# An S4 convolution block with a token-mixing MLP: the second token matrix and seven of eight pairs of the first in half-precision high and low parts, with a new order of all operations

## The chip, the cores and the metric

The kernel runs on one core of one Trainium2 chip. The core has a matrix engine (TensorE, PE in the profile, with its weight loads as PEld), a vector engine (VectorE, DVE), an activation engine (ScalarE, ACT), a general one (GpSimd, POOL) and SyncE (SP), which here only issues DMAs; sixteen DMA engines move the data. The metric is the device time of one execution in microseconds. It is the median of three runs.

## The reference, cut to what matters

The input `A_u` has 2048 tokens of 512 channels. It is normalized once, and the result goes two ways: through a long convolution along the tokens (an S4 layer, whose kernel is made from 128 complex states a channel), and through a mixer MLP whose first half mixes tokens by shifting.

```python
xn = layernorm(x)
s = irfft(rfft(pad(xn)) * rfft(pad(K))) + xn * Dskip      # K from A, B, C, log_dt
h = gelu(layernorm(xn) @ w1)                              # w1: 512 x 512
g0, g1, g2, g3 = h in four quarters of 128 channels, shifted by +1, -1, +2, -2 tokens
x1 = xn + concat(g0, g1, g2, g3) @ w2                     # w2: 512 x 512
h2 = gelu(layernorm(x1) @ w3) @ w4                        # 512 x 1376, 1376 x 512
out = x + s * silu(x1 + h2)
```

In this document w1 is the first token matrix and w2 the second.

## The kernel before, in words

**Tiling.** The tokens are dealt out in 16 steps of 128, so that a shift by one token is a change of the step: step `s` holds every sixteenth token from `s` on. `X` holds all 16 steps of 128 x 512 in SBUF as fp32 and is updated in place. Two neighbouring steps make a pair, and there are eight pairs.

**Token mixing** (`token_mixing`, line 1247). For each pair j, `ln_first` (1059) makes the statistics and normalizes the steps of `X`; `x_pair` (1080) scales them for the second normalization and brings them to channels by tokens; `h_pair` (1103) multiplies by w1 and applies the GELU; `u_stage1` (1125) does the first stage of the convolution's transform of the same steps and stores it to DRAM (`scr_Ud`). Pairs below `HF` (line 49, 4) work in fp32: TensorE transposes the scaled step `x2`, a copy brings it from PSUM to `xT`, and `w1s`, the raw w1, is the weight. The other pairs work in fp16: `x2` is cast to a high part, the rest `x2 - high` is the low part, a transposing DMA makes `xT`, and three matmuls stand for one product: high by high, high by low, low by high (`PASSES`, 839). For this `first_weights` (1030) squares w1, makes a power-of-two scale of it through TensorE and VectorE (`pow2_scale`, 978) and splits the scaled w1 into `w1h`. The GELU results of all pairs are kept in fp32 in `hT`; `wrapped` (1146) makes the six blocks `hw` whose shift leaves the step range.

`hs_pair` (1159) then does two steps at a time: four fp32 matmuls of 128 x 128 by 128 x 512 a step (`hT` or `hw` with the raw w2, `w2s`), and VectorE adds the sum from PSUM to `X` and takes the statistics of the result.

**The MLP** (`mlp`, 1203) runs over eight pairs in `MLP_ORDER` and six blocks of w3 columns (2 x 128, the last 96). It always works in fp16 parts: a matmul group of 12 into bank `pb`, the GELU into `g32`, a high part (`E.affine`) and a low part (`scalar_tensor_tensor`) into `ghl`, and groups of 6 into bank `pa`, which collect w4's products of the pair. `prep` splits w3 and w4, whose scales come from `weight_scales` (1020).

**The convolution.** `tables` (818) builds the convolution kernel K for 32 channels at a time, 16 times: exponentials, sines and cosines on ScalarE (`waves`), large products on VectorE (`sums`), matmuls, and the first stage of its transform (`ks`), which is stored to DRAM as `scr_Kfa` (channels 0 to 255) and `scr_Kfb` (256 to 511) through one buffer, `k1e`. `products` (841) takes half of the channels at a time: loads `cst` (transform constants), `uin` and `kin`, does the second stage, multiplies the spectra, goes one stage back and stores `scr_Zda` or `scr_Zdb`. For the second half both inputs are split into fp16 parts (`uh`, `kx`; stages `uhalf` and `khalf`). It needs all of `scr_Kfb`. `inverse` (947) loads these as `zin`, does the last stage and multiplies it into `X`, which `gate` (941) has passed through SiLU; `finish` adds the residual `xr` and stores the output.

**What sets the order.** No loop order is kept. Every operation is recorded with its number, in the order in which the source makes it (`Plan.new`, 249); operations inside `together` count as one. The text `ORDER` (116 to 199) lists all 1952 numbers, and `Plan.issue` (327) issues them in that order, each to its engine, where they run in order. Operations made by `E` (`Either`, 409) can run on ScalarE or VectorE; a letter behind the number says which (`a` or `v`). In this list MLP groups, tables, products and token mixing are woven into one another. Since all operations are issued from one place, almost every row of the profile has line 330, and rows are told apart by their tiles. Tiles come from rings and fixed places of SBUF: `wtile` (four buffers of 2 KB) serves `x2`, `x2h`, `x1n`, `x1h` and `g32`, and a new tile in a buffer waits for the readers of the old one.

Of the kernel before, what the change touches and what calls it, by code (L numbers as in the profile page):

```python
# [19 lines left out]
P = 128  # L20
L = 2048
D = 512
# [26 lines left out]
HF = 4  # L49
# [67 lines left out]
23 20 21 0 22 39 7 8 1 6 5 105 86 3 2 106 107 108 109 110 111 112 87 89 88 90 113 91 114 115a 92 93 94 95 25 24  # L117
26 27 116a 96 97a 1070 98v 117a 120v 99v 100 101a 102v 103 118 172 170 4 168 171 169 173 9 104a 10 19 18 11 28
166 167 174 175 176 121 123 124 177 178 122v 119a 125 145 44 179 180v 183v 146 46 126 127 128 181a 147 47 48
187a 208a 142 31 29 30 182v 129 78 205a 130 148 79a 153a 184v 228 229 230 131 143 160 185 35 34 33 32 132 232  # L120
133 149v 154a 231 144 186a 188 134 552 226 189a 233 193 150a 227 234 235 135 236 237 194 161 196 190 293 553 295
294 291 238 14 292 297 155 156 13 16 15 191 239 298 296 138a 240 299 244v 300 140a 301 202a 242a 302 141 554
241v 303 201a 49 245v 50 209 195 206 52 51 304 246a 247 53 54 192 152 17 151 380 382 203 249a 214 207a 250a 197a
198a 305 215 211 212 12 199 204 200 157 251 139 56 216 55 210a 59 45 80 217 243v 57 555 381 307a 272a 213 383 58
60 253 254 306a 81a 61 164 218a 62 36 252 223a 219a 384 248 308v 273v 222a 158 63 274 255 67 268v 162 68 64 256
257 220 225 259 276 221 224 275 565 277 314v 269a 69 270 70 136 137 71 557 258 65 261a 260a 279 265a 315v 278 66
264a 316 388 309v 72 280 282 73 271 337v 310a 311v 74 84 312 262 263 281 284v 283v 318 75 560 562 319 333v 317
266 267 338v 287a 76 339 313 288a 77 321 322 85v 334v 323 324 335 285 286 42 82 586 558 320 344 83a 345 556 385
559 566 567 340 326a 325a 289 346 389 336 341 290 330a 329v 43 37 328 327 568 359 360 587 561 347 588 331 349v
571 159 348v 40 332 163 353v 352v 350 351 361 375 378 446 374 570 448 390 342 355 569 377 572 449 563 564 362  # L130
354 41 363v 394 592 468 450 364a 589 438 591 386 590 391 470 471 396 439 574 573 440 343 576 575 387 443 454 577
578 595 593 165 441 579a 395 367a 397 392 356 376 357 456 455 400 402 607 393 594 404 608 442 358 366 398 457
580 472 581 582a 583a 597 459 584 403 596 613 372 609 401 447 368a 369 451 399 416 610 611 460 598 452 599 405
417 444 365 406 371 435 418 585 612 600a 628 370 616 629 458 630 469 473 419 474 601 38 407 475 453 462 432 614
631 633 632 480 495 602 420 408 603a 604a 461 615 409 634 421 410 445 411 379 499 476 605 606 657 412 618 422
413 477 617 478 414 373 482 423 637 424 479 425 494 481 463a 544a 635 433a 545a 464 415 619 620 502 621a 485
548a 549a 546 636 622 426 491 434 649 428 550 436a 650 496 659 660 547 465 466a 503 517 516 437 639 654 521 651
504 661 638 430 551 467 653 652 492a 746 623 747 488 489a 518 507 624a 490 662 748 510 493 655 513 749a 861 753
# [293 lines left out]
def kernel(  # L432
# [814 lines left out]
    def token_mixing():  # L1247
        V.memset(ssq, 0.0)
        for j in range(8):
# [16 lines left out]
            if j == 0:  # L1266
                for k in range(3, 6):
                    wrapped(k)
# [90 lines left out]
```

## Time and profile before

| | |
|---|---|
| median of three runs | 536.88 us (535.1 to 538.08) |
| span of the profiled execution | 536.6 us |
| busy: TensorE, VectorE, ScalarE | 516.5, 489.8, 425.2 us |
| ACT_TABLE_LOAD on ScalarE | 52, 66.7 us |
| DMA | 93.50 MB, mean 174 GB/s |
| granted TensorE clock, mean | 0.994 |

In a row of groups stand the line, the engine and the operation, then the tiles (written<-read), partitions x elements and type, the count; behind the first bar the busy time in us and the mean ns of one; behind the second bar the idle time of the engine just before them and what ended it. In the chain of work that ended last a piece has its start, its length and what it was; in a table of stages each engine's busy time stands with its number of instructions, then the granted TensorE clock, the mean share of the DMA engines that was busy, and the rate.

### The profile page before, as it was taken

What the parts mean: (1) busy time and instruction counts of PE and PEld (TensorE: products, weight loads), DVE (VectorE), ACT (ScalarE), POOL (GpSimd) and SP (SyncE); (2) the same over time, 40 slices, a digit from 0 to 9 for tenths busy, and PEclk for the clock granted to TensorE, in tenths of its full rate; (3) what the DMA queues carried; (4) which work ended last, traced back from release to release, by engine and by line L of the source; (5) the groups of instructions that cost most, each with busy time, mean ns of one, the idle gap of its engine ahead of it and who ended that gap; (6) DMA issues with size and microseconds to landing.
All of it is one profiled execution on the core that took longest, in us unless ns stands there. A gap on an engine that the chain in (4) does not pass through costs nothing.

```text
span 536.6 us, 13619 instructions
## 1 busy us (share of the span) xinstructions
PE 516.5 (96%) x5628; PEld 332.4 (62%) x5628; DVE 489.8 (91%) x755; ACT 425.2 (79%) x692; POOL 0.7 (0%) x6
## 2 busy tenths in 40 slices
PE   8999999999999999999999999999899899999992
PEld 7787664554475766565765666575565667666631
DVE  4999999999999999999999999999877799997277
ACT  3999999899899999999799897868646566774340
POOL 0000000000000000000000000000000000000000
PEclk9999999999999999999999999999999999999997
DMA  8989975689677325356375738838889969896997
GB/s 228 214 268 257 230 200 155 190 132 127 158 188 118 46 36 60 42 68 112 120 137 148 150 108 167 145 94 176 149 170 169 348 201 297 261 280 226 314 277 205
DMA packets 212830, 93.50 MB, mean 174 GB/s; under 512 B 163297, under 2 KB 196065, under 8 KB 212385
## 3 DMA queue, kind: packets, MB, share of 16 engines
q1 hardware_dynamic: 208032, 88.18, 71.3%
q10 hardware_dynamic: 4736, 4.46, 2.8%
q8 instruction: 44, 0.72, 0.6%
q14 instruction: 18, 0.14, 0.1%
HBM read 56.96 MB, written 29.36 MB: 161 GB/s over the span
## 4 chain that ended last, share of the span: by engine, by line
PE 63%; DVE 12%; ACT 11%; DMA 7%; issue 3%; SPq 1%; DVEq 0%; ACTq 0%
PE pb L330 24%; PE pa L330 17%; PE pd L330 11%; PE pc L330 11%; DVE wv L330 4%; DMA scr_Kfb<-k1e 3%; DVE X L330 3%; ACT wv L330 2%; ACT mag L330 2%; ACT L330 2%; SPq L330 1%; DMA kin<-scr_Kfb 1%; DMA scr_Kfa<-k1e 1%; DMA cst<-c_gq 1%; ACT g L330 1%
## 5 line engine op out<-in xcount | busy, mean ns | idle before, releaser
L330 PE MATMUL pb<-x1T,w3h 128*128 128x256 f16 (+1 forms) x1056 | 125.1, 273 | 1.2 <-ACT g L330 1.2
L330 PE MATMUL pa<-w4h,ghl 128*128 128x512 f16 (+1 forms) x528 | 123.2, 380 | 0.0
L330 PEld LDWEIGHTS <-w3h 128*128 128x128 f16 (+1 forms) x1056 | 102.3, 100 | 27.8 <-issue 11.0
L330 PEld LDWEIGHTS <-ghl 128*128 128x128 f16 (+1 forms) x528 | 49.3, 98 | 59.1 <-issue 8.7
L330 ACT ACT_TABLE_LOAD x52 | 66.7, 1283 | 2.0 <-PEq L1347 1.2
L330 ACT ACTIVATE wv<-wv 128x2080 f32<-128x2080 int32 x32 | 63.0, 1968 | 0.3 <-DVE wv L330 0.3
L330 ACT ACTIVATE g<-pb,wsc 128x512 f32<-128x512 f32 (+1 forms) x48 | 30.6, 651 | 12.8 <-PE pb L330 11.5
L330 ACT ACTIVATE ghl<-g,wsc 128x512 f16<-128x512 f32 (+1 forms) x39 | 26.6, 688 | 13.3 <-PE pa L330 8.3
L330 DVE TENSOR_TENSOR wv<-wv,eg 128x2048 f32<-128x2048 f32 x16 | 36.5, 2284 | 0.1
L330 DVE TENSOR_TENSOR wv<-mag,wv 128x2048 f32<-128x2048 f32 x16 | 36.6, 2285 | 0.0
L330 PE MATMUL pd<-pr,cst 64*128 64x256 f32 x256 | 36.3, 402 | 0.0
L330 PEld LDWEIGHTS pc<-wv 128*32 128x32 f32 x2048 | 29.8, 109 | 9.7 <-issue 6.2
L330 PE MATMUL pc<-wv 128*32 128x64 f32 x2048 | 32.5, 220 | 2.7 <-issue 1.9
L330 DVE SCALAR_TENSOR_TENSOR ghl<-g,wsc,ghl 128x512 f16<-128x512 f32 (+1 forms) x48 | 33.5, 701 | 1.0 <-ACT ghl L330 0.8
L330 ACT ACTIVATE wv<-wv,halfpi 128x2080 f32<-128x2080 f32 x16 | 32.9, 2056 | 0.1
L330 ACT ACTIVATE mag<-par 128x128 f32<-128x128 f32 x132 | 32.8, 441 | 0.0
L330 ACT ACTIVATE kh<-pc,ksc 128x256 f32<-128x256 f32 (+1 forms) x40 | 20.1, 553 | 14.1 <-PE pc L330 12.5
L330 PEld LDWEIGHTS pd<-pr,cst 64*128 64x128 f32 x256 | 22.0, 186 | 11.5 <-issue 8.3
L330 PE MATMUL pb<-xT,w 128*128 128x256 f32 x128 | 29.0, 382 | 0.0
L330 PEld LDWEIGHTS pb<-xT,w 128*128 128x128 f32 x128 | 23.8, 190 | 5.5 <-issue 1.6
L330 PE MATMUL pb<-w,hT 128*128 128x512 f32 x58 | 26.9, 599 | 0.0
L330 DVE BATCH_NORM_STATS2 stats<-X 128x6 f32<-128x512 f32 x32 | 21.4, 681 | 5.3 <-DMA X<-in_A_u_dram 5.3
(167 smaller groups left out, 882.7 us busy)
## 6 DMA issues: line engine op xcount, KB each, us to landing
wst<-in_B_w_dram SPq DMA_DIRECT2D x20, 512.0 KB, 4.0
scr_Ud<-ue SPq DMA_DIRECT2D x32, 256.0 KB, 3.2
scr_Kfa<-k1e SPq DMA_DIRECT2D x16, 256.0 KB, 6.2
uin<-scr_Ud SPq DMA_DIRECT2D x16, 256.0 KB, 4.1
cst<-c_gp SPq DMA_DIRECT2D x16, 256.0 KB, 3.5
kin<-scr_Kfa SPq DMA_DIRECT2D x16, 256.0 KB, 3.6
scr_Zda<-z1e SPq DMA_DIRECT2D x16, 256.0 KB, 3.0
scr_Kfb<-k1e SPq DMA_DIRECT2D x16, 256.0 KB, 6.0
```

Of the source, the lines that this page charges most:

```text
L330: ins = [getattr(self.engines[op.eng], name)(*args, **kw).ins for name, args, kw in op.calls]
```

## The change

`HF` goes from 4 to 1, so that pairs 1 to 3 also run in fp16 parts. The input's parts are made straight from `X`: the high part is the scaled step written as fp16, the low part one `scalar_tensor_tensor` from `X`; the fp32 `x2` remains for pair 0 only. Each GELU block of `h_pair` goes to a scratch tile `h32` in the ring `wtile`, and its high and low fp16 parts (scaled by `sh`) go to `hT`, which keeps its size; `hw` likewise. `second_weights` scales and splits w2 into `w2h`, whose raw copy is loaded into two slots of `sblocks` instead. `hs_pair` does 12 fp16 matmuls a step in place of 4 in fp32, and its add to `X` also takes the scale back. Steps 0 and 1 are loaded and normalized singly. With 56 operations more (2008), `ORDER` is a new list throughout, in which the letters differ as well: of the operations that may run on either engine, copies to `ue` on VectorE are 1 (before: 9), to `kh` 2 (11), to `z1e` 10 (17), normalizations of `X` 3 (9).

```diff
-HF = 4
+HF = 1
...
-23 20 21 0 22 39 7 8 1 6 5 105 86 3 2 106 107 108 109 110 111 112 87 89 88 90 113 91 114 115a 92 93 94 95 25 24
...
+12 2 3 27 0 90 8 7 5 6 25 91 92 93 94 26 95 24 115 4 117 118 116 119 120 10 23 48 13 121 96 122 97 98 11 9 100 123 124
+101 102 22 50 99a 109v 110 103 104 125 14 134 135 105 51 52 106 107 111a 136 137 17 20 126a 82 108a 56 138 112a 139 19
...
-    hw = at(gtile.o, [P, 6, P], F32, "hw")
+    hw = at(gtile.o, [P, 6, 2, P], F16, "hw")
...
     def loads():
...
-        by_r(X[:, 0:2], xv[:, :, 0:2], load=(Q, A))
+        by_r(X[:, 0:1], xv[:, :, 0:1], load=(Q, A))
+        by_r(X[:, 1:2], xv[:, :, 1:2], load=(Q, A))
...
-        load_w(w2, w2s, w2place, Q)
+        load_w(w2, w2s, Slots(sblocks + 10 * K4, sblocks + 11 * K4), Q)
...
         for r in range(4):
...
-    s3, i3, s4, i4, sg, ig, a3, a4, s1, i1, a1 = [wsc[:, k : k + 1] for k in range(11)]
+    s3, i3, s4, i4, sg, ig, a3, a4, s1, i1, a1, s2, i2, a2, sh = [
+        wsc[:, k : k + 1] for k in range(15)
+    ]
...
     def weight_scales():
...
-        pow2_scale(ssq[:, 8:16], s4, i4, 2.0 ** 14)
+        pow2_scale(ssq[:, 8:14], s4, i4, 2.0 ** 14)
...
-    w1h = []
+    w1h, w2h = [], []
...
     def first_weights():
...
+        V.tensor_scalar(sh, s1, 2.0 ** -10, None, op0=ALU.mult)
         for k in range(2):
...
+    def second_weights():
+        due("wq2")
+        for k in range(2):
+            w = wides[2 + k]
+            A.activation(at(phB + 4 * K4, [P, 2, D], F32, "sq"), w, AF.Square, accum_out=ssq[:, 14 + k : 15 + k])
+        pow2_scale(ssq[:, 14:16], s2, i2, 2.0 ** 14)
+        V.tensor_scalar(a2, i2, i1, 2.0 ** 10, op0=ALU.mult, op1=ALU.mult)
+        for k in range(2):
+            w = w2place([P, 2, 2, D], F16, "w2h")
+            E.affine(w[:, :, 0], wides[2 + k], s2)
+            V.scalar_tensor_tensor(w[:, :, 1], wides[2 + k], s2, w[:, :, 0], op0=ALU.mult, op1=ALU.subtract)
+            w2h.append(w)
...
     def prep(jp):
...
         for i in range(2):
...
-            x2 = wtile([P, D], F32, "x2")
-            E.affine(x2, X[:, s], r12[:, s, 1:2])
+            r2 = r12[:, s, 1:2]
...
-                E.copy(xh[:, 0], x2)
-                V.tensor_sub(xh[:, 1], x2, xh[:, 0])
+                E.affine(xh[:, 0], X[:, s], r2)
+                V.scalar_tensor_tensor(xh[:, 1], X[:, s], r2, xh[:, 0], op0=ALU.mult, op1=ALU.subtract)
...
+            x2 = wtile([P, D], F32, "x2")
+            E.affine(x2, X[:, s], r2)
...
                 for k in range(4):
...
     def h_pair(j):
-        h = stile([P, 4, 2, P], F32, "hT")
+        h = stile([P, 4, 2, 2, P], F16, "hT")
...
         for m2 in range(2):
...
-            hv = h[:, 2 * m2 : 2 * m2 + 2].rearrange("p m a t -> p m (a t)")
-            A.activation(hv, ph, AF.Gelu_apprx_tanh, scale=1.0 if j < HF else a1)
+            hv = [h[:, 2 * m2 : 2 * m2 + 2, k].rearrange("p m a t -> p m (a t)") for k in range(2)]
+            h32 = wtile([P, 2, 2 * P], F32, "h32")
+            A.activation(h32, ph, AF.Gelu_apprx_tanh, scale=1.0 if j < HF else a1)
+            E.affine(hv[0], h32, sh)
+            V.scalar_tensor_tensor(hv[1], h32, sh, hv[0], op0=ALU.mult, op1=ALU.subtract)
...
     def u_stage1(s):
...
     def wrapped(k):
...
-        src, dst = hT[s // 2][:, m, s % 2], hw[:, k]
+        src, dst = hT[s // 2][:, m, :, s % 2], hw[:, k]
...
-            V.tensor_copy(dst[:, 32:P], src[:, 0:96])
-            V.tensor_copy(dst[:, 1:32], src[:, 96:127])
-            V.memset(dst[:, 0:1], 0.0)
+            V.tensor_copy(dst[:, :, 32:P], src[:, :, 0:96])
+            V.tensor_copy(dst[:, :, 1:32], src[:, :, 96:127])
+            V.memset(dst[:, :, 0:1], 0.0)
...
-            V.tensor_copy(dst[:, 0:96], src[:, 32:P])
-            V.tensor_copy(dst[:, 96:127], src[:, 1:32])
-            V.memset(dst[:, 127:P], 0.0)
+            V.tensor_copy(dst[:, :, 0:96], src[:, :, 32:P])
+            V.tensor_copy(dst[:, :, 96:127], src[:, :, 1:32])
+            V.memset(dst[:, :, 127:P], 0.0)
...
     def hs_pair(s0, k):
...
                 for m in range(4):
...
-                        w = hT[t // 2][:, m, t % 2]
+                        w = hT[t // 2][:, m, :, t % 2]
...
-                    T.matmul(acc[i], w, w2s[m], start=m == 0, stop=m == 3)
+                    for n, (lh, lw) in enumerate(PASSES):
+                        T.matmul(
+                            acc[i], w[:, lh], w2h[m // 2][:, m % 2, lw],
+                            start=m == 0 and n == 0, stop=m == 3 and n == 2,
+                        )
         for i in range(2):
...
-            V.tensor_add(X[:, s], X[:, s], acc[i])
+            V.scalar_tensor_tensor(X[:, s], acc[i], a2, X[:, s], op0=ALU.mult, op1=ALU.add)
...
         for j in range(8):
...
             if j == 0:
-                ln_first(slice(0, 2))
+                ln_first(slice(0, 1))
+                ln_first(slice(1, 2))
...
             if j == 0:
                 for k in range(3, 6):
...
+        second_weights()
         for k in range(3):
...
         for i in range(12):
...
```

More of the change, by code (lines that the diff above doesn't have):

```diff
@@ L122 @@
[L122 to L131, printed above, removed]
@@ new lines @@
+1348 760 1362 576 761 543 762 1349 1363 1357 1367 1379 732a 565 1380 557 1368a 1369 746 1374a 763 1375 733 1364 1370
+747 749 734 1371 764 903 704 735a 736a 737 1376 738 765 750 769 766 1377 751 592 752 781 753a 754 1386 1387 593 594
+596 755 1381 1382a 1388 1389a 1378 756a 757a 758 595 782 1400a 1383 1401a 783 767 759 1390 1393 1394 1395 768 1408
+1409 1384 1402 784 1385 1415 785 1396a 1404a 786 1391 770 771 772 773 1392 774a 1397 597 1403 787 790 775 776 1405a
+788 1127 1406 1410 1128 789 1416 777a 1129 1411a 1131 778a 780 1412 1417 1422 791 1398 1399 1423 1413 1414 1137 1138
@@ L199 @@
+1900 1902 1908 1926 1951 1911 1598 1599 1905 1907 1968 1615 1605 1616v 1610v 1611 1617 1887 1914 1916 1906 1606 1915
[4 rows of a table added]
 """
```

132 lines of the change are left out of this document (65 added, 67 removed), and 11 rows, old and new, of the table ORDER.

## The prediction

> **What bounds the kernel now.** I read the page's busy times first, then the busy times by stage, then the chain that ended last.
>
> ```profile
> PE 516.5 (96%) x5628; PEld 332.4 (62%) x5628; DVE 489.8 (91%) x755; ACT 425.2 (79%) x692; POOL 0.7 (0%) x6
> ```
>
> TensorE is the fullest engine, VectorE is close behind, and an average over the span can't say which of them sets the end. So the stages:
>
> ```profile
> core 0: us, PE busy (x) PEld busy (x) DVE busy (x) ACT busy (x) POOL busy (x), PEclk, DMA share, GB/s
> 0.00:20.00 20.00, 17.09 (x117) 16.00 (x118) 12.25 (x46) 10.61 (x19) 0.70 (x6) 1.00 0.95 236
> 20.00:100.00 80.00, 79.05 (x629) 53.70 (x628) 78.02 (x152) 79.56 (x141) 0.00 (x0) 1.00 0.79 209
> 100.00:406.70 306.70, 302.15 (x3686) 187.28 (x3684) 298.70 (x397) 266.16 (x425) 0.00 (x0) 1.00 0.66 125
> 406.70:418.80 12.10, 12.06 (x92) 8.04 (x90) 6.21 (x22) 6.79 (x10) 0.00 (x0) 1.00 1.25 219
> 418.80:489.00 70.20, 68.78 (x703) 47.28 (x703) 65.61 (x88) 48.43 (x86) 0.00 (x0) 1.00 0.84 264
> 489.00:536.60 47.60, 37.40 (x410) 20.08 (x407) 28.97 (x55) 13.63 (x15) 0.00 (x0) 0.93 0.91 267
> 418.00:422.00 4.00, 2.63 (x29) 1.60 (x30) 3.64 (x5) 2.39 (x4) 0.00 (x0) 1.00 1.01 398
> 504.00:508.00 4.00, 4.00 (x30) 2.90 (x29) 0.28 (x1) 1.99 (x3) 0.00 (x0) 1.00 1.11 334
> 528.00:532.00 4.00, 0.99 (x16) 0.31 (x16) 3.96 (x10) 0.00 (x0) 0.00 (x0) 0.79 0.81 233
> ```
>
> Up to 406.7 us, where the last store of the convolution's stage-one spectrum is issued (the front), TensorE and VectorE are both over 97% busy, and from 20 to 100 us ScalarE is too. From 418.8 to 489 (the second half's products) TensorE is full with VectorE behind it. Behind 489 (the tail) TensorE still has MLP groups, and the transfers run at a share of 0.91. Between front and products stands a chain of transfers:
>
> ```profile
> 394.40 6.44 DMA scr_Kfb<-k1e
> ...
> 402.93 9.37 DMA scr_Kfb<-k1e
> ...
> 412.35 5.86 DMA kin<-scr_Kfb
> ```
>
> Its 12.1 us are spent in TensorE on MLP groups, which is why the TensorE share hides it.
>
> **TensorE: what goes.**
>
> ```profile
> L330 PE MATMUL pb<-xT,w 128*128 128x256 f32 x128 | 29.0, 382 | 0.0
> L330 PE MATMUL pb<-w,hT 128*128 128x512 f32 x58 | 26.9, 599 | 0.0
> L330 PE MATMUL pa<-w,hT 128*128 128x512 f32 x58 | 26.1, 594 | 0.0
> L330 PE MATMUL pb<-xT,w1h 128*128 128x256 f16 x192 | 22.0, 272 | 0.6 <-ACT hT L330 0.3 <-DMA xT<-x2h 0.3
> L330 PE MATMUL pd<-ident,x 128*128 128x128 f32 x32 | 4.3, 278 | 1.6 <-DVE x L330 1.3 <-ACT xT L330 0.2
> L330 PE MATMUL pa<-w,hw 128*128 128x512 f32 x6 | 3.1, 592 | 0.0
> L330 PE MATMUL pb<-w,hw 128*128 128x512 f32 x6 | 3.1, 592 | 0.0
> ...
> L330 PE MATMUL pa<-w4h,ghl 128*128 128x512 f16 x480 | 111.8, 380 | 0.0
> ```
>
>
> The second token matrix takes 26.9 + 26.1 + 3.1 + 3.1 = 59.2 us in fp32. In three half-precision passes it is 16 steps x 12 matmuls; at the MLP's 111.8 / 480 = 0.233 us for the same shape that is 44.7 us: 14.5 less. A pair of the first matrix is 29.0 / 4 = 7.25 us in fp32 and 22.0 / 4 = 5.5 us in fp16; three pairs change: 5.2 less. Of 32 transposes 24 go: 3.2 less. The new scale of w2 adds three instructions, under 1 us. TensorE ends 22 us lighter, at about 494.
>
> **VectorE and ScalarE: what comes.**
>
> ```profile
> L330 DVE SCALAR_TENSOR_TENSOR ghl<-g,wsc,ghl 128x512 f16<-128x512 f32 x40 | 29.7, 745 | 0.9 <-ACT ghl L330 0.8
> L330 ACT ACTIVATE ghl<-g,wsc 128x512 f16<-128x512 f32 x33 | 23.8, 722 | 13.3 <-PE pa L330 8.3 <-DVE X L330 3.4 <-DMA cst<-c_gq 1.4
> L330 DVE TENSOR_SCALAR ghl<-g,wsc 128x512 f16<-128x512 f32 x7 | 3.3, 477 | 0.9 <-PE pa L330 0.9
> L330 DVE SCALAR_TENSOR_TENSOR w1h<-w,wsc,w1h 128x1024 f16<-128x1024 f32 x2 | 2.6, 1280 | 0.0
> L330 ACT ACTIVATE w1h<-w,wsc 128x1024 f16<-128x1024 f32 x2 | 2.2, 1134 | 0.0
> L330 ACT ACTIVATE sq<-w 128x1024 f32<-128x1024 f32 x2 | 2.1, 1064 | 0.0
> L330 DVE TENSOR_SCALAR wsc<-wsc 128x1 f32<-128x1 f32 x10 | 1.5, 146 | 0.0
> L330 DVE TENSOR_TENSOR x2h<-x,x2h 128x512 f16<-128x512 f32 x8 | 5.5, 689 | 0.0
> L330 DVE CAST x2h<-x 128x512 f16<-128x512 f32 x5 | 2.1, 423 | 0.0
> L330 ACT CAST x2h<-x 128x512 f16<-128x512 f32 x3 | 1.8, 616 | 0.0
> L330 ACT COPY xT<-pd 128x512 f32<-128x512 f32 x7 | 3.9, 590 | 0.7 <-PE pd L330 0.7
> L330 DVE COPY ue<-pa 128x512 f32<-128x512 f32 x6 | 4.0, 685 | 0.0
> L330 DVE TENSOR_SCALAR X<-X,rs,bs 128x512 f32<-128x512 f32 x9 | 4.8, 543 | 0.1
> L330 DVE TENSOR_SCALAR kh<-pc,ksc 128x256 f32<-128x256 f32 x7 | 3.2, 476 | 0.2 <-ACT kh L330 0.2
> L330 DVE COPY z1e<-pd 128x256 f32<-128x256 f32 x17 | 7.0, 420 | 2.7 <-PE pd L330 2.7
> ```
>
> Each of the 16 GELU blocks of h_pair now gets a high part and a low part. The MLP's ghl is the same form: low parts 16 x 0.745 = 11.9 us on VectorE; high parts, by the letters in the order, 10 on ScalarE (7.2) and 6 on VectorE (2.9). For w2: low parts 2 x 1.28 = 2.6, high parts about 2.2, squares 2.1, and some ten one-column steps at 0.146, 1.5. Inputs of the first matrix: 14 low parts at 0.745 come (10.4); 8 subtractions (5.5), 8 casts (3.9) and 6 copies of xT at 0.59 (3.5) go: 2.5 less. The add in hs_pair takes a scale along: up to 1 us in all, taken as 1. Sum: 11.9 + 10.1 + 8.4 - 2.5 + 1 = 29 us, all ahead of the last table, where both engines are full. The letters push other work to ScalarE: off VectorE go 8 ue (5.5), 6 X (3.3), 9 kh (4.3), 7 z1e (2.9) and a few more, so VectorE gains only about 5 and ScalarE 24. The two single first steps should let the first normalization begin about 1 us earlier (0 to 2).
>
> **What the order moves.**
>
> ```profile
> 505.95 1.29 PE pa L330 x6
> 507.25 1.31 PE pb L330 x12
> ```
>
> ```profile
> L330 ACT ACTIVATE X<-X 128x1024 f32<-128x1024 f32 x8 | 8.3, 1053 | 4.9 <-DVE X L330 4.8
> ```
>
> Each number in ORDER is an operation in the order in which the source makes them, so the two lists can be read by stage. 47 MLP matmul groups (of 12 or 6 matmuls) stand behind the last spectrum store before and 23 after. A group in a row of groups takes about 1.3 us in the chain. So the front gets 24 groups, 31 us of TensorE, and with them 7 GELUs, 6 high and 6 low parts (19 at some 0.7: 13 us), four gates at 1.05 (4.2) and eight steps of norm and add near 0.7 (5.6): 23 us of VectorE and ScalarE.
>
> Front, before: VectorE 12.25 + 78.02 + 298.70 = 389, ScalarE 356, TensorE 398 us busy. After: TensorE 398 - 22 + 31 = 407; VectorE and ScalarE together 745 + 29 + 23 = 797, by the letters 405 and 392. VectorE still leads. At the 97.5% that 78.02 of 80 shows, the front takes 20 + (405 - 12.3) / 0.975 = 422.8 us; the same sum for before gives 406.4, as measured. Less the earlier start: 421.8, so 15 us **later** than now.
>
> New waits stand in the front too. Pairs 1 to 3 now need w1's scaled parts and a transposing DMA each where they needed copies of xT; in TensorE's list the next pairs and the u_stage1 blocks are queued behind them, and ScalarE's GELUs wait for those. hs_pair needs the scale of w2, a chain of small steps between VectorE and TensorE, with the updates of X behind it. I cost these at nothing because TensorE has room: its own sum for the front is 20 + (407 - 17.1) / 0.988 (79.05 of 80) = 414.6, 8 us ahead of VectorE's. Beyond 8 us of stall, or where VectorE is starved by one, each us counts in full. Six more transposing DMAs and four more X loads pass through SP's queue ahead of the stores of u and the later weight loads; the front's transfer share of 0.66 to 0.79 leaves room.
>
> Middle: the last store and load set it, with five groups beside them in both lists: 12.1 us, unchanged (a store alone took 6.44 or 9.37, so 3 us either way). Products: 22 groups stand there before, 8 after: TensorE 68.8 - 18 = 51, VectorE 65.6 - 11 = 54.5 (their splits and adds). At VectorE's present 65.61 / 70.2 that is 58.5 us. The transfers (264 x 70.2 = 18.5 MB) would need 311 GB/s; the best row has 398. I take 59.5. Tail: 10 groups in place of 20: TensorE 37.4 - 13 = 24, off the path. What remains is 267 x 47.6 = 12.7 MB; at the 334 GB/s of 504 to 508 that is 38.0; I take 38.5.
>
> Sum: 421.8 + 12.1 + 59.5 + 38.5 = 531.9 against the span of 536.6, or 4.7 less; on the median of 536.88 that is **532 us**.
>
> **The rivals.**
> *Slower: the transfers take TensorE's place.* Behind 418.8 the kernel moves 31.2 MB. My forecast wants 98 us for it, 318 GB/s on average. For it speak 398 and 334 GB/s in single rows; against it that whole stages ran at 264 and 267 with shares of 0.84 and 0.91, so full shares would give only 314 and 293, or 59 + 43 us. If the rates stay as they are, 421.8 + 12.1 + 117.8 = 552; halfway, 542. It turns into a loss where the average stays under 31.2 MB / 102.7 us = 304 GB/s. The Trainium skill ("DMA: Bandwidth & Descriptors", "Where 436 GB/s comes from") puts the HBM limit of one core at about 358 GB/s; by that figure 31.2 MB would need 87 us at least, and the 398 of 418 to 422 stands above it. Chance 0.22.
> *No change: an even trade.* Full shares, 102 us, just pay for the front: 536. Chance 0.20.
> *Much faster: the front does not grow.* If VectorE's and ScalarE's additions fell into gaps, TensorE's 22 us would come off: 514. Against it: VectorE's 97.5% from 20 us on. Chance 0.04.
> *A cold TensorE.* In the tail TensorE will have 24 us of work in 38.5, so it idles in pieces. The row of 528 to 532, where it is idle three parts in four, shows a granted clock of 0.79. Were it at half the clock for the whole tail, its 24 us would be 48, 9.5 past the tail: 541. Against it: 14 us of idle time in many pieces leave few of several us. The Trainium skill ("TensorE: Matmul & The Clock Gate", Part 1) says that an idle window of about 3.4 us halves the clock; that row agrees in direction. Chance 0.04.
>
> **How the numbers follow.** My forecast has 0.50. About 0.5% is what a measurement of this kernel can tell from no change, 534.2 to 539.6 us. Forecast and much faster lie under it: 0.54. Above lie the transfer case and the cold one: 0.26. The even trade is the same: 0.20. The range: at 99% for VectorE, as ScalarE's 79.56 of 80, the front is 416 and the end 526; with the tail at 398 GB/s (32 us) 520. Above, the transfer case halfway, 542, and a front at 96%, 6 us more on my forecast, 538. I take 521 to 543.
>
> **What would show it.** Right: TensorE about 494 busy, VectorE 494, ScalarE 449; the last store of the spectrum near 422 us; from there under 111 us with GB/s above 310; in the late chain VectorE and DMA in place of TensorE's pa and pb. Wrong: the store before 415 or behind 430 (the sum of the front), a late part of 118 us or more at the old rates (the transfers), or TensorE still filling the products.

## The result, and the profile after

The changed kernel takes 564.45 us (median of 4 runs, 562.69 to 568.28) beside 537.48 us for the kernel before (4 runs, 535.1 to 540.35): a ratio of 1.050, 95% interval 1.044 to 1.056. It is **slower by 27 us**. The forecast was 532 us, its range 521 to 543.

The page of the changed kernel, first busy time by engine, then the stages (columns as in the tables above). The stages are cut as in the prediction: where the issue of the last `scr_Kfb` store ends, at 443.1 us (before: 406.9); the cuts are 442.9 and 406.7.

```profile
PE 508.9 (90%) x5719; PEld 329.5 (58%) x5719; DVE 496.1 (88%) x764; ACT 451.2 (80%) x735; POOL 0.7 (0%) x6
```

```profile
core 0: us, PE busy (x) PEld busy (x) DVE busy (x) ACT busy (x) POOL busy (x), PEclk, DMA share, GB/s
0.00:20.00 20.00, 15.85 (x98) 14.55 (x99) 11.37 (x43) 11.62 (x19) 0.70 (x6) 0.94 0.90 227
20.00:80.00 60.00, 51.90 (x434) 36.74 (x434) 51.01 (x118) 49.17 (x82) 0.00 (x0) 0.91 1.03 246
80.00:100.00 20.00, 20.00 (x132) 12.72 (x130) 19.86 (x40) 19.09 (x46) 0.00 (x0) 1.00 0.73 211
20.00:100.00 80.00, 71.90 (x563) 49.47 (x563) 70.87 (x157) 68.25 (x127) 0.00 (x0) 0.93 0.96 237
100.00:442.90 342.90, 330.65 (x4102) 211.05 (x4099) 325.31 (x433) 314.77 (x492) 0.00 (x0) 1.00 0.57 113
442.90:456.10 13.20, 10.18 (x67) 5.16 (x65) 9.87 (x24) 6.68 (x8) 0.00 (x0) 1.00 1.06 233
456.10:520.50 64.40, 54.11 (x588) 37.51 (x592) 53.34 (x63) 41.00 (x84) 0.00 (x0) 0.97 0.85 269
520.50:564.30 43.80, 26.19 (x318) 11.76 (x312) 25.36 (x48) 8.86 (x9) 0.00 (x0) 0.76 0.97 287
```

Two things are to be seen. The busy times of VectorE (496 for 494) and ScalarE (451 for 449) are close to the forecast's: their work was counted rightly. TensorE's 509 for 494 is 15 us more; its granted clock is 0.91 to 0.97 in the rows up to 80 us and in the products, and 0.76 in the tail. But from 20 to 100 us no engine is full any more. Before, VectorE was busy 97.5% of 20 to 100 us; here it is 70.87 of 80, or 89%, and TensorE and ScalarE, which could have been the bound in its place, are at 90% and 85%: all three wait. The idle time lies ahead of 80 us; from 80 to 100 us VectorE is busy 19.86 of 20.

| stage (us) | before | forecast | after |
|---|---|---|---|
| front, to the last spectrum store | 406.7 | 421.8 | 442.9 |
| middle | 12.1 | 12.1 | 13.2 |
| products of the second half | 70.2 | 59.5 | 64.4 |
| tail | 47.6 | 38.5 | 43.8 |
| span | 536.6 | 531.9 | 564.3 |

What the engines wait for in the front is told by the chain that ended last. These are its shares and some of its pieces from 270 to 442 us in the changed kernel, where tables and the first half's products alternate:

```profile
by line: PE pa L328 19.3%; PE pd L328 18.8%; PE pb L328 15.8%; PE pc L328 9.3%; SPq L328 7.2%; DMA kin<-scr_Kfa 4.6%; DMA scr_Kfa<-k1e 4.2%; DMA scr_Kfb<-k1e 3.9%; DMA uin<-scr_Ud 3.8%; DMA cst<-c_gp 2.9%; DMA x1T<-x1h 2.3%; issue 2.0%; ACT
```

```profile
274.65 7.25 DMA scr_Kfa<-k1e
282.04 2.80 DMA kin<-scr_Kfa
...
297.95 4.92 DMA cst<-c_gp
...
377.97 3.48 SPq L328
...
382.94 6.75 DMA scr_Kfb<-k1e
...
391.50 2.64 SPq L328
394.18 5.05 DMA kin<-scr_Kfa
...
421.34 3.87 DMA x1T<-x1h
...
435.08 6.61 DMA uin<-scr_Ud
```

Transfers take 21.7% of this stretch and the queue of SyncE, which issues them (SPq), another 7.2%: 29% of 172 us, or 50 us in which the chain hangs on a store, a load or on the queue ahead of it. This is where the chain runs and not time that is lost: behind 100 us VectorE is still busy 325.31 of 342.9 us. The stretch from 270 to 403 us of the kernel before (a piece that crosses the edge of a stretch counts whole, so shares can add up to more than 100%):

```profile
by line: PE pd L330 24.9%; PE pb L330 23.5%; PE pa L330 23.2%; PE pc L330 13.6%; DMA scr_Kfb<-k1e 11.9%; issue 2.3%; SPq L330 1.4%; ACT mag L330 1.4%; ACT g L330 1.0%; ACT L330 1.0%; DVE k1e L330 0.6%; ACT x1n L330 0.5%; ACT ghl L330 0.5%; 
```

There the only transfers on the chain are the last two stores of the spectrum; 85% of it is TensorE. So in this stretch the chain of the kernel before ran through TensorE, and not through VectorE, by which the prediction reckoned the front.

### The profile page after: what moved, and what is told of

Same layout as the page of the kernel before. It is cut to its first block, busy times and chain, and to the rows that moved or that the text cites. A ratio compares the mean times of both kernels' runs of the same rounds, so it can differ in the third digit from the quotient of the medians.

```text
span 564.3 us, 13881 instructions
## 1 busy us (share of the span) xinstructions
PE 508.9 (90%) x5719; PEld 329.5 (58%) x5719; DVE 496.1 (88%) x764; ACT 451.2 (80%) x735; POOL 0.7 (0%) x6
## 4 chain that ended last, share of the span: by engine, by line
PE 40%; DMA 19%; ACT 6%; DVE 2%; SPq 2%; issue 2%; DVEq 0%; ACTq 0%
PE pa L328 12%; PE pb L328 11%; PE pd L328 9%; PE pc L328 9%; DMA cst<-c_gq 4%; DMA kin<-scr_Kfb 2%; SPq L328 2%; DMA scr_Kfb<-k1e 2%; DMA zin<-scr_Zda 2%; DMA x1T<-x1h 2%; DVE X L328 2%; DMA kin<-scr_Kfa 1%; ACT wv L328 1%; ACT mag L328 1%; DMA scr_Kfa<-k1e 1%
## 5 line engine op out<-in xcount | busy, mean ns | idle before, releaser
L328 PE MATMUL pb<-x1T,w3h 128*128 128x256 f16 (+1 forms) x1056 | 123.3, 273 | 3.2 <-DMA x1T<-x1h 2.2
L328 PE MATMUL pa<-w4h,ghl 128*128 128x512 f16 (+1 forms) x528 | 121.1, 380 | 0.0
L328 PE MATMUL pb<-xT,w1h 128*128 128x256 f16 x336 | 40.7, 283 | 4.9 <-DMA xT<-x2h 3.7
L328 PEld LDWEIGHTS <-w1h 128*128 128x128 f16 x336 | 33.5, 101 | 15.6 <-issue 9.2
L328 ACT ACTIVATE kh<-pc,ksc 128x256 f32<-128x256 f32 (+1 forms) x47 | 22.8, 547 | 11.7 <-PE pc L328 9.5
L328 PEld LDWEIGHTS <-cst 128*64 128x64 f16 x384 | 19.9, 111 | 20.5 <-issue 12.5
L328 PEld LDWEIGHTS <-hT 128*128 128x128 f16 x174 | 16.9, 98 | 19.9
L328 ACT ACTIVATE ghl<-g,wsc 128x512 f16<-128x512 f32 (+1 forms) x35 | 24.1, 695 | 3.9 <-issue 1.7
```

The costliest lines, as they stand in the source:

```text
L328: ins = [getattr(self.engines[op.eng], name)(*args, **kw).ins for name, args, kw in op.calls]
```

## The experiments

All ratios are to the kernel before on the same chip, with 95% intervals; the median of before was 537 to 540 us in every set. Two theories stood against each other. **A**: the 29 us of VectorE and ScalarE work that the change adds made the loss. **B**: its new order made it.

**1 and 2. The change, and its second matrix alone, in the order of before.** Every operation that both kernels have keeps its place; the new ones stand right behind what they need.

```diff
...
+            if j == 3:
+                second_weights()
             due(f"h{j}")
             h_pair(j)
...
-        second_weights()
```

> The whole change, but in the order of before: every operation that both kernels have stands where it stood, the new ones right behind the ones they need, and w2's scale and parts are made behind pair 3 instead of behind pair 7. Theory A (the added 29 us of VectorE and ScalarE work in the front set the loss): the work is all here, so most of the 27 us stay: 550 to 560. Theory B (the new order sets it, by bunching the token mixing and its transfers in the first 80 us and by bringing the MLP groups out of the products): little stays: 535 to 545, and the stage from 20 to 80 us is full on VectorE as before.

> Only the second token matrix in half-precision parts (GELU parts, w2's scale and parts, three passes), pairs 1 to 3 of the first matrix as before, in the order of before. Added: 26 us of VectorE and ScalarE; removed: 14.5 us of TensorE. Theory A: half of 26, near 13 us, comes on top: about 550. Theory B: TensorE's saving and the new work cancel: 533 to 542.

Measured: 595.96 us (1.105, 1.099 to 1.110) and 585.45 us (1.089, 1.083 to 1.095). Both are slower than the changed kernel itself and lie outside the ranges of both theories: they are 57 and 47 us above the kernel before, where 29 and 26 us of work were added. From 20 to 100 us of the first:

```profile
20.00:100.00 80.00, 45.52 (x297) 31.52 (x296) 54.11 (x132) 47.08 (x72) 0.00 (x0) 0.76 0.66 162
```

VectorE is busy 54 of 80 us. Its longest wait there is for ScalarE (8.7 us, for a part of `x2h`), and TensorE waits 7.2 us for `w1h` from VectorE. This fits new operations that stop what stands behind them in a list that runs in order on each engine. So neither run tells A from B. They tell how much an order weighs: the same operations, 94 of them on the other of their two engines, take 564 us in one and 596 in another.

**3. The changed kernel with pairs 1 to 3 through TensorE again.**

```diff
-HF = 1
+HF = 4
...
+            if j < 3:
+                due("xp0b" if j == 0 else f"xp{j}")
+                x_pair(j + 1)
```

> The changed kernel with pairs 1 to 3 of the first token matrix back in fp32 through TensorE transposes (6 transposing DMAs fewer in the first 80 us, 7 to 8 us more of TensorE), the rest of the new order as it is. If the transposing DMAs make the idle time of the stage from 20 to 80 us: 5 to 8 us less than the changed kernel, 557 to 560. If that idle time is there because the new order has no other work beside the chain of the token mixing: no gain or a loss, 564 to 570.

Measured: 585.48 us (1.087, 1.082 to 1.093).

```profile
20.00:100.00 80.00, 66.31 (x414) 47.31 (x413) 50.09 (x115) 50.39 (x85) 0.00 (x0) 0.88 0.59 161
```

The share of the DMA engines falls from 0.96 to 0.59, and VectorE idles more, not less. Its longest waits in these 80 us are for TensorE (what it waits for: us in all, times, longest):

```profile
DVE xT L327 <- PE pd L327: 16.0, 2, 10.4
```

The copies of `xT` wait 16 us for TensorE's transposes, which pairs 1 to 3 of the changed kernel do not have. So whatever relief there was is lost to waits of the same kind as in runs 1 and 2, and the run does not tell whether the transposing DMAs made the idle time of this stage in the changed kernel.

**4. One part alone on the kernel before: the input's parts straight from `X`, pairs 4 to 7.**

```diff
-            x2 = wtile([P, D], F32, "x2")
-            E.affine(x2, X[:, s], r12[:, s, 1:2])
...
-                E.copy(xh[:, 0], x2)
-                V.tensor_sub(xh[:, 1], x2, xh[:, 0])
+                E.affine(xh[:, 0], X[:, s], r2)
+                V.scalar_tensor_tensor(xh[:, 1], X[:, s], r2, xh[:, 0], op0=ALU.mult, op1=ALU.subtract)
```

> The kernel before with one part of the change: the half-precision parts of the first matrix's inputs (pairs 4 to 7) are made straight from X, so eight scaling steps of 0.5 to 0.7 us on VectorE and ScalarE go, 5 us in all. Theory A (VectorE and ScalarE bound the front): 2 to 3 us less, 534 to 535. If TensorE bounds the front: no difference, 537.

Measured: 539.56 us (1.001, 0.998 to 1.004): no difference. Eight steps less on the two engines that looked full bring nothing in an order made for the old ones. By its expectation, this is also what a front would show that TensorE bounds.

**5 and 6. The changed kernel in another order, and the control.** Both orders come from the kernel's own by many small moves, each kept where the sum over the durations of the traces came out earlier. Of the operations that may run on either engine 57 and 77 changed theirs.

```diff
 ORDER = """
-12 2 3 27 0 90 8 7 5 6 25 91 ...
+3 7 6 8 1126 90 5 12 0 4 13 43 ...
...
```

> The changed kernel's operations, all of them and with their engines nearly as they are, in another order: made from the changed order by many small moves, each kept where a sum over the traces' own durations, with 0.7 us more for each transfer in half of its cases, came out earlier. Nothing is left out. Theory B (the order of the change is what costs, because its chains run through transfers with no other work beside them): 20 us or more of the 27 come back, 525 to 545. Theory A (the added VectorE and ScalarE work costs whatever the order): little comes back, 553 to 564.

> The control: the kernel before, its operations untouched, its order treated in the same way as the changed kernel's in the run beside this one. If the treatment alone gains, it shows here: 522 to 533. If the order of before is as good as it gets: 535 to 540. What the change itself is worth, orders being equal, is the difference between the run beside this one and this one: theory A 15 us or more, theory B 0 to 8.

Measured: 547.06 us (1.013, 1.006 to 1.020) for the change, 545.08 us (1.011, 1.009 to 1.014) for the control. **The same operations as the change's, 17 us faster, by another order**; the engines' sums hardly move with it (VectorE 494.2 us beside 496.1, ScalarE 451.8 beside 451.2). The control came out slower than the kernel before, so this way of ordering is worse than the one that made that kernel; a likely reason is told under "What was not expected". Treated alike, the change and the kernel before differ by 2 us, with intervals that overlap. So most of the loss is the order's, as theory B has it, though run 5 ends 2 us above the range that B was given. In the reordered change:

```profile
core 0: us, PE busy (x) PEld busy (x) DVE busy (x) ACT busy (x) POOL busy (x), PEclk, DMA share, GB/s
0.00:20.00 20.00, 18.23 (x122) 16.12 (x123) 12.37 (x51) 12.79 (x22) 0.70 (x6) 1.00 0.91 238
20.00:100.00 80.00, 69.91 (x556) 47.66 (x555) 77.12 (x173) 73.72 (x134) 0.00 (x0) 0.96 0.93 252
100.00:427.50 327.50, 325.86 (x4064) 205.41 (x4061) 317.19 (x405) 310.69 (x487) 0.00 (x0) 1.00 0.58 113
427.50:437.20 9.70, 8.73 (x57) 4.81 (x57) 6.02 (x15) 2.30 (x6) 0.00 (x0) 1.00 0.92 229
437.20:502.10 64.90, 53.76 (x604) 37.47 (x608) 55.66 (x69) 43.47 (x88) 0.00 (x0) 1.00 0.89 285
502.10:544.30 42.20, 27.81 (x330) 11.94 (x328) 25.83 (x48) 8.82 (x9) 0.00 (x0) 0.79 0.98 297
```

The front ends at 427.5 us, 15 earlier; VectorE behind 20 us is busy 77.12 + 317.19 = 394.3 of 407.5 us, or 96.8%. And its chain from 270 us to the last store:

```profile
by line: PE pb L327 25.6%; PE pd L327 23.8%; PE pa L327 22.1%; PE pc L327 13.8%; DVE wv L327 5.9%; DVE pr L327 1.2%; issue 1.2%; ACT L327 0.8%; DVE up L327 0.7%; DVE eg L327 0.7%; ACT wv L327 0.7%; ACT k1e L327 0.7%; DVE x1h L327 0.5%; ACT 
```

Not one transfer is left on it, where the changed kernel had 29% with their queue. 85% of it is TensorE, which behind 100 us is busy 325.86 of 327.5 us, more than VectorE's 317.19.

**7. The parts that only take work away, ordered in the same way** (parts straight from `X` for pairs 4 to 7, steps 0 and 1 singly, on the kernel before).

```diff
-        by_r(X[:, 0:2], xv[:, :, 0:2], load=(Q, A))
+        by_r(X[:, 0:1], xv[:, :, 0:1], load=(Q, A))
+        by_r(X[:, 1:2], xv[:, :, 1:2], load=(Q, A))
...
-                ln_first(slice(0, 2))
+                ln_first(slice(0, 1))
+                ln_first(slice(1, 2))
```

> Two small parts of the change on the kernel before (pairs 4 to 7: half-precision parts made straight from X; steps 0 and 1 loaded and normalized singly), the second matrix and pairs 1 to 3 as before, order treated in the same way. Both parts take work or waiting away and add none: 1 to 4 us less than the control beside this run, if the front is bound by VectorE and ScalarE; no difference if TensorE is the bound.

Measured: 542.95 us (1.006, 1.003 to 1.009), 2.1 less than the control, as was expected of a front bound by VectorE and ScalarE, but the intervals of the ratios overlap slightly. If the two parts bring something where the order is made anew, it is not enough to beat the kernel before.

**8 and 9. What sets the second half's products.** In the changed kernel the chain through this stage, its shares and some pieces:

```profile
by line: DMA cst<-c_gq 38.9%; DMA kin<-scr_Kfb 21.8%; PE pc L328 21.0%; PE pd L328 20.3%; DMA scr_Zdb<-z1e 7.2%; PE pb L328 4.2%; DVE pr L328 1.9%; issue 1.9%; DVE z1e L328 0.7%; DVE kx L328 0.1%; SPq L328 0.0%; DVEq L328 0.0%
```

```profile
476.21 5.21 DMA cst<-c_gq
481.42 0.04 issue
481.47 1.50 PE pc L328 x24
482.97 1.09 PE pd L328 x8
484.05 0.02 issue
484.07 5.34 DMA cst<-c_gq
```

Each load of `cst` starts when the last matmul (`pd`) of an earlier unit has let go of one of its two buffers, and the next unit waits 5 us for it. That reads as a buffer too few; or the load is slow because the DMA engines are busy. Run 8 gives it a third buffer, one of the four of `pr`, and lets the loads of units 2 to 7 stand one unit earlier in the list; run 9 leaves out the loads for units 2 to 7, which then use the constants of units 0 and 1.

```diff
...
-            uin=Ring(late, K4, 3), cst=Ring(late + 3 * K4, K4, 2), kin=Ring(late + 5 * K4, K4, 3),
-            pr=Ring(o, K4, 4), kh=Ring(o + 4 * K4, K4, 2), z1e=Ring(o + 6 * K4, K4, 3),
+            uin=Ring(late, K4, 3), cst=Cycle(late + 3 * K4, late + 4 * K4, o + 3 * K4), kin=Ring(late + 5 * K4, K4, 3),
+            pr=Ring(o, K4, 3), kh=Ring(o + 4 * K4, K4, 2), z1e=Ring(o + 6 * K4, K4, 3),
```

```diff
+            if not hf or un < 2:
+                cst = ring["cst"]([P, nb, 2, 2, P], F32, "cst")
...
+                csts[un % 2] = cst
+            cst = csts[un % 2]
```

> The changed kernel with a third buffer for cst in the second half's products (taken from pr, which keeps three), so that each load of cst can be issued one unit earlier; nothing else is moved. If the two buffers set the pace of that stage (each load waits until a unit's last matmul is through): 4 to 6 us less than the changed kernel, 558 to 560. If the rate of the transfers sets it: no difference, 562 to 566.

> The changed kernel with six of the eight loads of cst in the second half's products left out (units 2 to 7 use the constants of units 0 and 1), so 3.1 MB less are moved in that stage; matmuls and order as they are. If the rate of the transfers sets the stage: 3.1 MB at the stage's 269 GB/s is 11.7 us at most; the work of VectorE there is 53.3 of 64.4 us, so 5 to 9 us less are left to gain, 555 to 559. If it is set by the chain of each unit or by the engines: 0 to 2 us less, 562 to 565.

Measured: 564.61 us (1.044, 1.037 to 1.052) and 558.18 us (1.038, 1.034 to 1.043). With the third buffer the chain of the stage is

```profile
by line: PE pd L327 25.5%; PE pc L327 25.4%; DMA kin<-scr_Kfb 24.5%; DMA cst<-c_gq 17.1%; PE pb L327 6.5%; PE pa L327 4.4%; ACT z1e L327 2.1%; DVE pr L327 1.9%; issue 1.7%; SPq L327 0.5%; DVE kx L327 0.1%; DVEq L327 0.0%
```

The wait for `cst` halves, TensorE's and `kin`'s shares grow, and the whole time does not move by more than the runs can tell. The stage from its first split (`khalf`, unit 0) to its last copy takes 67.3 us in the profile of the changed kernel, 63.6 in that of run 8, and in run 9, with 3.1 MB less, 58.4; in this order:

```profile
453.20:520.50 67.30, 54.97 (x596) 38.09 (x603) 55.99 (x66) 41.00 (x84) 0.00 (x0) 0.97 0.85 269
```

```profile
452.10:515.70 63.60, 56.63 (x596) 39.28 (x603) 55.66 (x66) 40.82 (x84) 0.00 (x0) 0.95 0.87 275
```

```profile
451.80:510.20 58.40, 54.62 (x596) 38.17 (x603) 55.30 (x66) 41.00 (x84) 0.00 (x0) 0.97 0.77 249
```

So the buffers have a part in this stage, up to 4 us, and the loads themselves a larger one, 9 us. Run 9 takes the waits for these loads away together with their bytes, so how much the bytes weigh by themselves is not shown. Of the 58.4 us that are left VectorE is busy 55.3.

**10 and 11. What VectorE's added work costs, and TensorE's saved work is worth**, both in the order of run 5. Run 10 makes each GELU low part twice, run 11 leaves out two of the three passes of the second matrix.

```diff
             V.scalar_tensor_tensor(hv[1], h32, sh, hv[0], op0=ALU.mult, op1=ALU.subtract)
+            V.scalar_tensor_tensor(hv[1], h32, sh, hv[0], op0=ALU.mult, op1=ALU.subtract)
```

```diff
-                    for n, (lh, lw) in enumerate(PASSES):
+                    for n, (lh, lw) in enumerate(PASSES[:1]):
...
-                            start=m == 0 and n == 0, stop=m == 3 and n == 2,
+                            start=m == 0 and n == 0, stop=m == 3 and n == 0,
```

> The changed kernel in its new treatment (all operations, other order), with each of the 16 GELU low parts made twice, one right behind the other: 11 to 12 us more of VectorE in the first 100 us, nothing else. If VectorE's work bounds the front whatever the order (theory A): 9 to 12 us more than without, 556 to 559. If there is room for it beside other work (theory B): 0 to 5 us more, 547 to 552.

> The same order, with two of the three half-precision passes of the second token matrix left out: 30 us less of TensorE, nothing else. If TensorE bounds that order too: 10 us or more less, below 538. If its savings fall into gaps, as VectorE's and ScalarE's work goes on beside it: 0 to 4 us less, 543 to 547, and then the 14.5 us that the change takes off TensorE in the second matrix are worth little as well.

Measured: 563.04 us (1.044, 1.040 to 1.049), 16 more than run 5; and 551.85 us (1.025, 1.020 to 1.030), 5 **more** than run 5, with intervals of the ratios that just touch. The second low parts are paid in full and over: the last GELU part of `h7` ends at 105.9 us in place of 92.0, 14 us later for 11.9 us of work. That is the answer of theory A, for work added to an order that is left as it is. But from 20 to 100 us VectorE is busy 74.04 of 80 us in run 10 and 77.12 in run 5, so stalls as in runs 1 and 2 have a part in it. The matmuls that run 11 leaves out (TensorE is busy 489.7 us in place of 504.3) are worth nothing, as the prediction said of its 22 us in the front. That it came out slower goes with a slower clock; from 100 to 120 us, where the second matrix runs, run 11 and then run 5:

```profile
100.00:120.00 20.00, 14.55 (x41) 5.62 (x42) 18.59 (x54) 19.91 (x46) 0.00 (x0) 0.66 0.50 157
```

```profile
100.00:120.00 20.00, 20.00 (x95) 9.13 (x93) 18.97 (x51) 19.91 (x42) 0.00 (x0) 1.00 0.44 134
```

ScalarE is busy 19.91 of 20 us in both, so TensorE's time is not what sets this stretch. The granted clock is 0.66 instead of 1.00, with TensorE idle for 5 of 20 us. The Trainium skill ("TensorE: Matmul & The Clock Gate", Part 1) has the clock halve after an idle window of about 3.4 us; these rows agree in direction, and what the slow clock cost by itself was not measured.

**12. A kernel meant to beat both**: parts straight from `X`, steps 0 and 1 singly, pair 3 in fp16, the second matrix in fp32, ordered anew with durations fitted to ten traces.

```diff
-HF = 4
+HF = 3
```

> A kernel meant to beat both: the kernel before with the parts of the change that add no work (half-precision parts straight from X, steps 0 and 1 singly) and with one pair more of the first matrix, pair 3, in half precision (HF = 3); the second matrix stays in fp32. Order from many small moves from the order of before, judged by durations fitted to ten of the traces. If the operations that the change adds for the second matrix are what made it worse: 528 to 535. If the order of before is hard to better: 536 to 543.

Measured: 542.14 us (1.008, 1.005 to 1.011). It does not beat the kernel before, as was expected of an order that is hard to better.

**13 to 18. Which part of the order.** The changed kernel with one stretch of its list in another order (13: 900 places; 14: places 916 to 1675; 17: the first 570; 18: the first 866), all of its operations from the order of before (15), and all in an order with as many groups behind the last store as run 5's (16). In each of them 11 to 83 of the operations that may run on either engine change theirs too. Run 16 was made with durations fitted to ten traces, 17 and 18 with those of run 5. For instance run 14:

```diff
-... 755 1381 1382a 1388 1389a 1378 756a 757a 758 595 782 1400a ...
+... 902 755 1381 1382a 1388 42 ...
...
```

> The changed kernel with only the first 900 of its 2008 places in another order (up to about 230 us: token mixing, weights, first tables); behind it every operation stands where the change put it. If the bunched token mixing with its transfers in the first 100 us makes the loss: 12 to 17 us less than the changed kernel, 547 to 553. If the loss is made later, where tables and the first half's products alternate: 0 to 6 less, 558 to 564.

> The changed kernel with only places 916 to 1675 in another order (about 230 to 460 us: tables 7 to 15 woven with the first half's products and MLP groups); the first 916 stand as the change put them. If the loss is made there, by tables and products that wait for the store and load of the same few buffers: 9 to 14 us less, 550 to 556. If it is made in the first 100 us: 0 to 5 less, 559 to 564.

> All operations of the change, order treated as before, but starting from the order of before, so that 48 MLP groups stand behind the last spectrum store (the change has 23). If bringing 24 groups into the front, and so fewer behind it, was itself a cost: 2 to 10 us less than the reordered change of the earlier run (547), 537 to 545. If it is worth something, as the forecast had it (4.7 us in all): 548 to 556.

> All operations of the change, its 23 groups behind the last store, treated longer and with durations fitted to ten traces. If the change's operations as such can pay: 530 to 537. If they are worth nothing on balance, at the best order found: 538 to 546. If the added VectorE work costs in any order: 547 or more.

> The changed kernel with only the first 570 of its 2008 places in another order (to about 130 us: token mixing, the weights' scales and parts), made with the durations that gave the first reordered change (547), 24 of the operations that may run on either engine changing theirs; all behind stands as the change put it. If that order of the first 130 us makes a good part of the loss: 6 to 10 us less than the changed kernel, 554 to 558. If it is not made there: 0 to 3 less, 561 to 565.

> The same for the first 866 places (to about 230 us), 28 operations changing their engine. If the loss is made in the token mixing and the first tables together: 11 to 17 us less than the changed kernel, 547 to 553. If it is mostly made behind 230 us, as the run with the middle alone would have it with its 5 us, more is not to be had here either: 558 to 564.

| run | what has another order | us | ratio |
|---|---|---|---|
| 13 | first 230 us | 576.01 | 1.067 (1.062 to 1.072) |
| 14 | 230 to 460 us | 559.55 | 1.038 (1.032 to 1.044) |
| 15 | all, from the order of before (48 groups behind the last store) | 555.39 | 1.030 (1.025 to 1.034) |
| 16 | all (23 groups) | 557.72 | 1.035 (1.029 to 1.041) |
| 17 | first 130 us | 567.95 | 1.056 (1.051 to 1.062) |
| 18 | first 230 us, durations of run 5 | 561.94 | 1.048 (1.040 to 1.055) |

Against the changed kernel's 1.050 (1.044 to 1.056) only run 14 among the single stretches gains, about 5 us; runs 17 and 18 do not differ from it, and 13 is worse, for a reason that is not shown. By their expectations run 14 speaks for the first 100 us (0 to 5 us gained) and run 18 for a loss behind 230 us (558 to 564). Runs 17 and 18 gain nothing clear of the noise and run 14 does, so a part of the loss seems to be made from 230 us on, where tables and products wait for stores and loads. Runs 15 and 16 gain 9 and 7 us, less than run 5's 17. Run 16 lies where its expectation puts a cost of the added VectorE work in any order (547 or more); but it has the same operations and as many groups behind the last store as run 5, so what it shows first is that orders made in this way scatter by more than 10 us. The single stretches don't add up to 17 us, and where the rest of run 5's gain lies stays open. Whether the 24 groups moved into the front pay is not settled either: run 15 keeps 48 behind the store and ends between runs 5 and 16.

## Why the prediction was wrong

**The work of the front: right.** To 442.9 us VectorE was busy 11.37 + 70.87 + 325.31 = 407.6 us (forecast 405), ScalarE 394.6 (392). TensorE had 418.4 (407), 11 more; the granted clock was 0.94 and 0.93 in the rows up to 100 us, which the forecast's durations did not have, and an estimate from these rows (busy time times what the clock lacks to 1.00) gives 6 of the 11. The earlier start came out at 0.6 us: the first normalization of `X` starts at 9.8 us in place of 10.5.

**"At the 97.5% that 78.02 of 80 shows": this step failed.** Behind 20 us VectorE was busy 396.2 of 422.9 us, 93.7%. At 97.5% that work would have ended at 426.4; 16.5 of the 21 us that the front missed are this share, 7 of them between 20 and 100 us and 9 behind; most of the rest is 3.5 us more of VectorE's work. The share was read from the order of before and carried over to a list that is new throughout. That such a share can be had for these operations is shown by run 5: 96.8%, front at 427.5.

**"I cost these at nothing because TensorE has room" and "the front's transfer share leaves room": the reason behind it, and it is the wrong kind of reason.** Room in the sums of an engine says nothing of a chain that goes from VectorE through SyncE's queue, a transfer, TensorE and ScalarE back to VectorE. From 20 to 80 us of the changed kernel, where VectorE is busy 51.01 of 60 us, these are among the longest waits (engine and tile, what it waits for: us in all, times, longest):

```profile
PEld pa L328 <- ACT ue L328: 4.6, 3, 4.0
DVE x2h L328 <- DMA xT<-x2h: 3.8, 2, 2.1
PE pb L328 <- DMA xT<-x2h: 3.7, 2, 2.0
ACT ue L328 <- DMA scr_Ud<-ue: 3.3, 3, 2.3
```

They hang together: the parts `x2h` wait for a buffer that a transposing DMA still reads, the matmuls `pb` for that DMA, `ue` for a store, and the next matmuls `pa` for `ue`. In run 5 the waits of `x2h` and `pb` for that DMA are gone and that of `ue` for its store is 1.2 us. TensorE's wait for `ue` is longer there (8.7 us), yet VectorE is busy 77.12 of the 80 us to 100: this wait by itself did not cost the share. That the tables come late is not the reason by itself either: the first `waves` are through at 113.9 us in the changed kernel and at 81.0 in the kernel before, but at 107.2 in run 5. Behind 270 us it is the stores and loads of the chain shown above, which are off the chain in run 5. That the order is what costs is shown by run 5; which wait costs how much is not, beyond run 14's 5 us.

**The middle: right within its 3 us** (13.2 for 12.1; run 5: 9.7).

**Products, 64.4 us for 59.5, and tail, 43.8 for 38.5: the rates.** The forecast wanted 311 and 334 GB/s of them, from single rows of 4 us; the stages ran at 269 and 287, the tail with the DMA engines busy at a share of 0.97. The rival "the transfers take TensorE's place" had put these two stages at 102 us with full shares and at 118 with the old rates; they took 108. For the products runs 8 and 9 fit this, with up to 4 us for the buffers of `cst`. In the best order of the change, run 5, they still took 64.9 and 42.2, so this part of the miss (10 us) is not the order's. It alone is more than the 4.7 us of gain: with the forecast's 421.8 and 12.1 us ahead of them, these two stages would have ended at 542 us, behind the 536.6 of before. The cold TensorE of the fourth rival came too, a clock of 0.76 in the tail, but its 26 us of work lie there beside transfers that fill the stage.

**VectorE leads, TensorE's savings are worth nothing in the front: shown for a part of it.** Run 11 shows it where the second matrix runs, up to about 120 us. Against it stand run 4, which found no difference, and the chains behind 270 us, 85% TensorE in the kernel before and in run 5. What a us of TensorE is worth there no run tried. The prediction did not have the slower clock that goes with a freed TensorE.

**The sum for the change as such.** Ordered alike, change and kernel before are 547.06 and 545.08: the 4.7 us of gain that the forecast had are not seen there, and no loss of 15 either; with runs 15 and 16 of the same operations at 555 and 558 us, one pair of orders does not settle what the operations are worth. So 17 of the 27 us came with the order. The mistake of sign did not come from the order alone, since the products and the tail missed by 10 us in run 5 too.

## What to carry to other kernels

A busy share belongs to an order, not to a stage: when a change brings a new list for engines that run in order, a sum of busy times gives a lower bound, and the chain through the transfers has to be followed in the new list, step by step, from the list itself. Take a stage's transfer rate from that whole stage and not from its best 4 us. And before a new operation is judged by its time, compare orders of equal care: here one set of operations took from 547 to 596 us.

## What was not expected of the hardware

A matmul group takes longer behind one of another shape. In run 5's chain a group `pa` of six takes 1.29 to 1.30 us behind another MLP group and 1.40 behind `pd` or `pc`, a group `pb` of twelve 1.31 and 1.42 (1.47 once in these rows):

```profile
281.48 1.31 PE pb L327 x12
282.79 1.29 PE pa L327 x6
284.09 1.06 PE pd L327 x8
285.18 1.47 PE pb L327 x12
286.65 1.88 PE pd L327 x16
288.53 1.42 PE pb L327 x12
289.94 1.30 PE pa L327 x6
...
293.20 1.06 PE pd L327 x8
294.26 1.40 PE pa L327 x6
```

That is 0.11 us for each change (the trace gives the shapes of `pd` and `pc` here as 64*128, 128*64, 128*32 and 32*64, the MLP's as 128*128, its last block 128*96 and 96*128). With rows and columns each taken as 32, 64 or 128, the control, run 6, changes its shape from one matmul to the next 245 times, the kernel before 188 times, and TensorE's busy time with the same 5628 matmuls is 525.3 us against 516.5:

```profile
PE 525.3 (96%) x5628; PEld 330.2 (61%) x5628; DVE 485.4 (89%) x740; ACT 432.6 (79%) x706; POOL 0.7 (0%) x6
```

8.8 us for 57 changes is 0.15 each, near the 0.11 of the rows; the mean granted clock, 0.991 beside 0.994, would by an estimate make up 1.6 of the 8.8. It is a likely reason why the control is slower than the kernel before; it was not tried by itself. The Trainium skill ("TensorEngine Tiling (Array Packing)", Key Properties) says that a change of the tiling mode drains TensorE; it gives no time for it. The rows above fit it.
